# The attention output transposed by DMA instead of TensorE, and the output projection's half-depth products gathered four tiles at a time

## The chip, the core and the metric

The kernel runs on one core of a Trainium2 chip. The metric is the device time of one execution in microseconds (us). Three runs of the kernel before gave a median of 173.98 us (173.03 to 174.68).

## What is computed

One transformer block with two parallel branches on 2048 rows of width 448: linear attention with 16 heads of 28 channels and a softmax feature map, and a two-layer feed-forward net with the Mish activation. Both read the same normalized rows, and the block adds both to its input.

```
xn = layernorm(x)                                 # x: 2048 x 448
q, k, v = split(xn @ wqkv)                        # 16 heads x 28
pq, pk = q @ w_phi, k @ w_phi                     # per head 28 x 28
phi_q = [softmax(pq), softmax(-pq)]; phi_k likewise
kv = phi_k^T v;  z = sum(phi_k)
o = (phi_q @ kv) / (phi_q . z + 1e-6)
A = concat_heads(o) @ wo                          # 448 x 448
B = mish(xn @ w1 + b1) @ w2                       # 448 -> 1792 -> 448
out = x + A + B
```

## The kernel before, in words

The 2048 rows are 16 tiles of 128 rows. Names: TensorE is PE, VectorE is DVE, ScalarE is ACT, GpSimd is POOL; SP only issues DMAs. The program is written in one order, and a small planner (`Prog.add`) gives each engine its own in-order stream and puts a semaphore wait where an instruction needs what another engine or a DMA has produced, or a buffer or PSUM bank that another one still uses. Each DMA has a semaphore of its own. Nothing is reordered: an engine that waits holds up all that stands behind it.

The width 448 is three and a half times 128. A product over 448 channels is therefore cut into four chunks that start at channels 0, 128, 192 and 320 (`C0`), so that chunks 1 and 2 overlap in 64 channels. A tile uses three full chunks (`full`, L321) and 64 rows of the fourth (`rem`, L326). For two tiles of opposite parity the two half-depth products lie in different halves of the PE array, rows 0 to 63 and rows 64 to 127, and run side by side in a row-tiled pass. Where such a product stands between full products the array changes its tiling and back.

Three stages follow one another. In the first, layernorm, projections, exponentials and the sums over keys are computed; pairs of tiles are transposed on the way, the first two pairs on PE, the other six by DMA transposes from the SP queue (`xT`, L172). In the second, a loop over n = 0 to 27, PE computes the hidden layer: each n gives 128 hidden channels for 1024 rows (`ffn1_full` and, at every even n for two values of n, `ffn1_rem`), and ACT applies Mish (L491). Woven in, from n = 5 on, is the attention of tile m = n - 5: `nd_mm` (L438) multiplies exponentials of the queries with the key sums into two PSUM banks, one for each half of the feature map. The second half has a single bank, 7, for all tiles; the first half alternates between 5 and 6. `nd` then runs five DVE operations per tile: a reciprocal (L446), a product (L447), t2 (L449, the last to read bank 7), t1 (L452) and the reciprocal of the denominator (L454). POOL multiplies (L455) into one of four buffers `o_sb`. `t1` has two buffers.

`oTr(j)` takes a pair of tiles: eight PE transposes (L314) into PSUM bank 4, each of a 128 x 128 chunk, and one ACT copy (L463) into `oT`. `oT` is the memory of `EqT`'s first half, whose query exponentials have been read by then. The loop calls `oTr(0)` at m = 3, and so on every second step to m = 17 (n = 22).

In the third stage, `final(j)` for eight pairs of tiles, PE adds the second feed-forward layer (`f1`, L504: 14 products of 128 hidden channels each for a tile) and the output projection (three `full` products with `Wo` for each tile, and one side-by-side pass of the two `rem` products) in one PSUM bank per tile. DVE adds x (L515) into `out_sb`, and SP issues the store.

Of the kernel before, what the change touches and what calls it, by code (L numbers as in the profile page):

```python
# [5 lines left out]
ACT = mybir.ActivationFunctionType  # L6
ALU = mybir.AluOpType
# [5 lines left out]
D = 448  # L13
H = 16
DH = 28
F = 1792
P = 128
NT = S // P
FC = F // P
# [127 lines left out]
def ap_on(src, dims):  # L147
    return bass.AP(tensor=src.tensor, offset=src.offset, ap=[list(src.ap[0])] + [list(d) for d in dims])


def bass_parallel_sum__linear_kernel_hedgehog__dense_activation_mish__prompt_kernel(
    nc, A_x, A_wqkv, A_w_phi, A_wo, B_x, B_w1, B_b1, B_w2, out
):
    with ExitStack() as es:
        _kernel(es, nc, A_x[0], A_wqkv, A_w_phi, A_wo, B_w1, B_b1, B_w2, out[0])


def _kernel(es, nc, x2, A_wqkv, A_w_phi, A_wo, B_w1, B_b1, B_w2, out2):
    KC, KP, QG = 4, 112, 4
    E1 = DH + 1  # L160
    E2 = DH + 2
    pr = Prog(nc, es)
    pe = lambda fn, **k: pr.add("PE", fn, **k)
    act = lambda fn, **k: pr.add("ACT", fn, **k)
    dve = lambda fn, **k: pr.add("DVE", fn, **k)
    pool = lambda fn, **k: pr.add("POOL", fn, **k)

    def dma(eng, out, in_, r=(), w=()):
        return pr.add(eng, lambda e: e.dma_start(out, in_), r=r, w=w, dma=True)

    def dma_t(eng, out, in_, r=(), w=()):
        return pr.add(eng, lambda e: e.dma_start_transpose(out, in_), r=r, w=w, dma=True)  # L172

    def sb(name, shape, dtype=BF16):
        return es.enter_context(nc.sbuf_tensor(name, shape, dtype))

    ident = sb("ident", [P, P])
# [5 lines left out]
    x_all = sb("x_all", [P, NT, D])  # L183
# [5 lines left out]
    W2 = sb("W2", [P, FC, D])  # L189
    Wo = sb("Wo", [P, KC, D])  # L190
# [11 lines left out]
    hm = [sb(f"hm{i}", [P, FC, 1024]) for i in range(2)]  # L202
# [7 lines left out]
    t1 = [sb(f"t1_{i}", [P, H, E1], FP32) for i in range(2)]  # L210
    t2 = [sb(f"t2_{i}", [P, H, E1], FP32) for i in range(2)]
    rden = [sb(f"rden{i}", [P, H], FP32) for i in range(2)]
    NO = 4
    o_sb = [sb(f"o_sb{i}", [P, D]) for i in range(NO)]
    oT = EqT[:, 0, :, :]
    out_sb = [sb(f"out_sb{i}", [P, D]) for i in range(3)]
    PS = es.enter_context(nc.psum_tensor("PS", [P, 8, 512], FP32))
    PSb = PS.bitcast(BF16).rearrange("p (b n) -> p b n", b=8) if len(PS.bitcast(BF16).shape) == 2 else PS.bitcast(BF16)

# [11 lines left out]
    def wk(key):  # L231
        return [key + "0", key + "1"]
# [16 lines left out]
    for base, cm, st in ((0, 1, -DH), (DH - 1, -1, DH)):  # L249
# [7 lines left out]
         r=["wraw", "mask"], w=["Wbd"])  # L257
# [53 lines left out]
    def transp(e, bank, src, u):  # L311
        for c in range(KC):
            o = c * 256 + u * P
            i = e.transpose(PSb[:, bank, o:o + P], src[:, C0[c]:C0[c] + P], ident[:])  # L314
        return i
# [3 lines left out]
    def full(e, out, lhs, rhs, u, start=True, stop=False):  # L319
        for n, c in enumerate(FULL[u]):  # L320
            i = e.matmul(out, lhs(ALLP, c), rhs(ALLP, c), start=(start and n == 0), stop=(stop and n == 2))  # L321
        return i

    def rem(e, out, lhs, rhs, u, start=False, stop=True):
        h = slice(HP * u, HP * (u + 1))
        return e.matmul(out, lhs(h, 1 + u), rhs(h, 1 + u), start=start, stop=stop)  # L326
# [23 lines left out]
    def sl(w):  # L350
        return lambda h, c: w[h, c, :]
# [79 lines left out]
    def nd_bank(t, s):  # L431
        return 7 if s else 5 + t % 2

    def nd_mm(t, s):
        b = nd_bank(t, s)
        def f(e):
            for g in range(QG):
                i = e.matmul(PS[:, b, g * QG * E2:(g + 1) * QG * E2], EqT[0:KP, s, g, t * P:(t + 1) * P],  # L438
                             KVZ[:, s, g, :, :], start=True, stop=True)
            return i  # L440
        pe(f, r=[f"Eq{t // 4}{gp}{s}" for gp in range(2)] + [f"KVZa{s}", "KVZ1"], x=[b])

    def nd(t):
        i = t % 2
        nds = [PS[:, nd_bank(t, s), 0:H * E2].rearrange("p (h c) -> p h c", c=E2) for s in range(2)]
        dve(lambda v: v.reciprocal(rq[i][:, 1, :], nds[1][:, :, E1]), w=[f"rq{i}"], x=[7])  # L446
        dve(lambda v: v.tensor_tensor(rq[i][:, 0, :], nds[0][:, :, E1], rq[i][:, 1, :], ALU.mult),  # L447
            r=[f"rq{i}"], w=[f"rho{i}"], x=[nd_bank(t, 0)])
        dve(lambda v: v.tensor_tensor(t2[i][:, :, :], nds[1][:, :, 0:E1],  # L449
                                      ap_on(rq[i][:, 0, 0:1], [[1, H], [0, E1]]), ALU.mult),  # L450
            r=[f"rho{i}"], w=[f"t2{i}"], x=[7])
        dve(lambda v: v.tensor_tensor(t1[i][:, :, :], nds[0][:, :, 0:E1], t2[i][:, :, :], ALU.add),  # L452
            r=[f"t2{i}"], w=[f"t1{i}"], x=[nd_bank(t, 0)])
        dve(lambda v: v.reciprocal(rden[i][:, :], t1[i][:, :, DH]), r=[f"t1{i}"], w=[f"rd{i}"])  # L454
        pool(lambda g: g.tensor_tensor(o_sb[t % NO][:, :].rearrange("p (h d) -> p h d", d=DH), t1[i][:, :, 0:DH],  # L455
                                       ap_on(rden[i][:, 0:1], [[1, H], [0, DH]]), ALU.mult),
             r=[f"t1{i}", f"rd{i}"], w=[f"o{t % NO}"])

    def oTr(j):
        for u in range(2):  # L460
            t = 2 * j + u
            pe(lambda e, t=t, u=u: transp(e, 4, o_sb[t % NO], u), r=[f"o{t % NO}", "ident"], x=[4])
        act(lambda a: a.activation(oT[:, :, 256 * j:256 * j + 256],  # L463
                                   PSb[:, 4, :].rearrange("p (c n) -> p c n", c=KC), ACT.Copy),
            w=[f"oT{j}"], x=[4])

    def fargs(n, u):
        tcp, fc = n // FC, n % FC
# [2 lines left out]
    def ffn1_full(n, u):  # L471
        tcp = n // FC
        first = n % 2 == 0
        pe(lambda e: full(e, *fargs(n, u), u, first, not first),
           r=wk("W1") + [f"xT{4 * tcp + 2 * u}", f"xT{4 * tcp + 2 * u + 1}"], x=[2 * (n % 2) + u])

    def ffn1_rem(n):
        for i in (n, n + 1):
            pe(lambda e, i=i: (rem(e, *fargs(i, 0), 0, i > n, i == n), rem(e, *fargs(i, 1), 1, i > n, i == n))[1],
               r=wk("W1") + [f"xT{4 * (i // FC) + u}" for u in range(4)], x=[2 * (i % 2), 2 * (i % 2) + 1])  # L480
# [10 lines left out]
        act(lambda a: a.activation(hm[tcp][:, fc, :].rearrange("p (u n) -> p u n", u=2), PS[:, b:b + 2, :], ACT.Mish,  # L491
                                   bias=b1T[:, fc:fc + 1]), r=["b1T"], w=[f"hm{tcp}"] + rr, x=[b, b + 1])

    OB = [5, 0, 1, 2, 3, 6]
    def final(j):
        bs = [OB[(2 * j + u) % len(OB)] for u in range(2)]
        def wo(u):
            t = 2 * j + u
            return PS[:, bs[u], 0:D], sl(oT[:, :, t * P:(t + 1) * P]), sl(Wo)
        def f1(e, u):  # L500
            t = 2 * j + u
            for fc in range(FC):
                o = (t % 8) * P
                i = e.matmul(PS[:, bs[u], 0:D], hm[t // 8][:, fc, o:o + P], W2[:, fc, :],  # L504
                             start=(u == 0 and fc == 0), stop=(u == 1 and fc == FC - 1))
            return i
        pe(lambda e: f1(e, 0), r=[f"hm{j // 4}", "W2"], x=[bs[0]])
        pe(lambda e: full(e, *wo(0), 0, False, False), r=[f"oT{j}"] + wk("Wo"), x=[bs[0]])
        pe(lambda e: (rem(e, *wo(0), 0), rem(e, *wo(1), 1, True, False))[1], x=bs)
        pe(lambda e: full(e, *wo(1), 1, False, False), x=[bs[1]])  # L510
        pe(lambda e: f1(e, 1), x=[bs[1]])
        for u in range(2):
            t = 2 * j + u
            i = t % 3
            dve(lambda v, u=u, t=t, i=i: v.tensor_tensor(out_sb[i][:, :], PS[:, bs[u], 0:D], x_all[:, t, :], ALU.add),  # L515
                r=[f"x{t}"], w=[f"out{i}"], x=[bs[u]])
            dma("SP", ov[:, t, :], out_sb[i][:, :], r=[f"out{i}"])

    NP = NT // 2
    NWARM = 48  # L520
# [22 lines left out]
    def ln_b(j):  # L543
# [4 lines left out]
       r=["ident"], x=[7])  # L548
# [43 lines left out]
    for n in range(2 * FC):  # L592
        m = n - KV_END - 2
        if n:
            ffn1_full(n, 0)
        if 0 <= m < NT:
            nd_mm(m, 0)
        if n:
            ffn1_full(n, 1)
        if n % 2 == 0:  # L600
            ffn1_rem(n)
        mish(n)
        if 0 <= m < NT:
            nd_mm(m, 1)
            nd(m)
        if n == 0:
            for j in range(4):
                kv_mm(j)
        if 4 + n < NP:
            kv_mm(4 + n)  # L610
        if n == KV_END:
            kvz()
        if m >= 3 and m % 2 == 1 and (m - 3) // 2 < NP:
            oTr((m - 3) // 2)
    for j in range(NP):
        final(j)
    pr.finish()


# [26 lines left out]
```

## Time and profile before

| what | value |
|---|---|
| median of three runs | 173.98 us |
| the profiled execution: time, span | 174.11 us, 172.1 us |
| PE busy | 163.7 us, 95% of the span |
| DVE, ACT, POOL busy | 85.3, 81.7, 52.8 us |
| the attention steps in the loop, first to last `nd_mm` | 67.7 to 102.6 us |
| third stage | 114.5 us to the end |

The span is the part of the execution in which instructions run; 2.0 us lie outside it. Busy time says how long an engine had an instruction in work. For PE it is not the same as progress, since its products overlap one another and their ends are modelled; the chain of work that ended last gives each piece the time by which it moves the end. PSUM appears as PS. Because `oT` lies in `EqT`, the profile names it EqT; W in the third stage is W2, and in the second W1.

### The profile page before, as it was taken

The numbers are of one execution on the slowest core, as the hardware profiler recorded it, in microseconds if no ns is written. First come the engines' busy times: TensorE is split into PE (matmuls) and PEld (weight loads), VectorE is DVE, ScalarE is ACT, GpSimd is POOL, SyncE is SP. The second block draws the span as 40 slices with busy tenths as digits, with TensorE's granted clock in tenths as the row PEclk, the third lists the DMA queues.
The fourth block names the chain that finished last, engine by engine and source line by source line (L and its number), as shares of the span: only waits on it lengthen the run. The fifth ranks groups of instructions, "written<-read, shape, count | busy, mean of one in ns | idle before, by whom it ended". The sixth has DMA issues, their size and how long they took to land.

```text
span 172.1 us, 2723 instructions
## 1 busy us (share of the span) xinstructions
PE 163.7 (95%) x1137; PEld 85.0 (49%) x1137; DVE 85.3 (50%) x166; ACT 81.7 (47%) x84; POOL 52.8 (31%) x54
## 2 busy tenths in 40 slices
PE   6859899999999999999999999999999999999993
PEld 6734344444346855455555554344454544544541
DVE  1674966999996003898888883001121112111211
ACT  2374599999989535567766668760000000000000
POOL 5424259556699900244444442000000000000000
PEclk9987999999999999999999999999999999999999
DMA  5994693349900000000000000000000100110110
GB/s 159 360 234 73 213 228 98 61 35 314 258 0 4 0 2 4 0 0 4 0 0 0 4 0 0 0 4 27 27 27 31 51 28 27 50 32 27 30 52 28
DMA packets 15628, 10.72 MB, mean 62 GB/s; under 512 B 9216, under 2 KB 14848, under 8 KB 15616
## 3 DMA queue, kind: packets, MB, share of 16 engines
q1 hardware_dynamic: 14432, 9.15, 20.1%
q10 hardware_dynamic: 1152, 1.40, 2.4%
q8 instruction: 9, 0.15, 0.4%
q14 instruction: 3, 0.02, 0.1%
q0 software_dynamic: 32, 0.00, 0.0%
HBM read 6.68 MB, written 1.84 MB: 49 GB/s over the span
## 4 chain that ended last, share of the span: by engine, by line
PE 79%; DVE 9%; DMA 6%; ACT 4%; issue 1%; ACTq 1%; DVEq 0%
PE PS L321 35%; PE PS L504 25%; PE PS L326 7%; PE PS L438 4%; DVE xn L279 4%; PE PS L412 4%; DMA Wk<-in_A_wqkv_dram 3%; DMA xnT<-xn 2%; DVE Sk L392 2%; PE PS L314 2%; DVE stats L266 1%; ACT EqT L403 1%; ACT hm L386 1%; DVE Wp L309 1%; ACT hm L293 1%
## 5 line engine op out<-in xcount | busy, mean ns | idle before, releaser
L504 PE MATMUL PS<-W,hm 128*128 128x448 bf16 x224 | 43.8, 352 | 0.0
L321 PE MATMUL PS<-xnT,W 128*128 128x512 bf16 x168 | 43.0, 379 | 0.0
L491 ACT ACTIVATE hm<-PS,b1T 128x1024 bf16<-128x1024 f32 x28 | 31.2, 1113 | 20.5 <-PE PS L326 11.6
L515 DVE TENSOR_TENSOR out_sb<-PS,x_all 128x448 bf16<-128x448 f32 x16 | 10.0, 625 | 55.1 <-PE PS L326 33.5
L504 PEld LDWEIGHTS PS<-W,hm 128*128 128x128 bf16 x224 | 21.9, 98 | 20.5
L395 POOL TENSOR_TENSOR hm<-hm,rSk 128x1792 bf16<-128x1792 bf16 x8 | 25.5, 3211 | 8.8 <-DVE rSk L394 8.8
L321 PEld LDWEIGHTS PS<-xnT,W 128*128 128x128 bf16 x168 | 14.5, 97 | 11.6 <-issue 1.2
L392 DVE TENSOR_REDUCE Sk<-hm 128x64 f32<-128x1792 bf16 x8 | 15.9, 1992 | 1.5 <-ACT hm L386 1.5
L403 ACT ACTIVATE EqT<-PS 112x1024 bf16<-112x1024 f32 x16 | 15.4, 1022 | 0.3 <-PE PS L326 0.3
L386 ACT ACTIVATE hm<-PS 128x896 bf16<-128x896 f32 x16 | 13.9, 932 | 0.9 <-PE PS L321 0.9
L438 PEld LDWEIGHTS PS<-KVZ,EqT 112*128 112x128 bf16 x128 | 9.0, 97 | 9.1 <-DVE t_0 L452 3.0
L455 POOL TENSOR_TENSOR o_sb<-t_0,rden 128x448 bf16<-128x448 f32 x8 | 7.5, 940 | 19.3 <-DVE rden L454 19.3
L321 PE MATMUL PS<-xnT,Wp 128*112 128x512 bf16 x48 | 12.0, 385 | 0.9 <-ACT Wp L307 0.7
L438 PE MATMUL PS<-KVZ,EqT 112*128 112x120 bf16 x128 | 12.1, 216 | 0.0
L321 PE MATMUL PS<-Wv,xnT 128*128 128x448 bf16 x48 | 11.4, 378 | 0.4 <-DMA xnT<-xn 0.4
L321 PE MATMUL PS<-Wo,EqT 128*128 128x448 bf16 x48 | 11.8, 354 | 0.0
L279 DVE TENSOR_SCALAR xn<-x_all,mv,rstd 128x512 bf16<-128x512 bf16 x16 | 10.8, 718 | 1.2 <-POOL rstd L274 1.2
L455 POOL TENSOR_TENSOR o_sb<-t_1,rden 128x448 bf16<-128x448 f32 x8 | 7.5, 941 | 11.2 <-DVE rden L454 11.2
L266 DVE BATCH_NORM_STATS2 stats<-x_all 128x6 f32<-128x448 bf16 x16 | 9.1, 611 | 3.7 <-DMA x_all<-in_A_x_dram 3.7
L321 PE MATMUL PS<-Wp,xnT 128*128 128x448 bf16 x48 | 10.7, 359 | 0.0
L532 ACT ACTIVATE v_ext<-PS 128x896 bf16<-128x896 f32 x8 | 7.4, 919 | 5.5 <-PE PS L326 5.5
L321 PEld LDWEIGHTS PS<-xnT,Wp 128*112 128x112 bf16 x48 | 5.7, 129 | 6.7 <-ACT EqT L403 2.7
(62 smaller groups left out, 151.5 us busy)
## 6 DMA issues: line engine op xcount, KB each, us to landing
W<-in_B_w_dram SPq DMA_DIRECT2D x2, 896.0 KB, 5.3
out_dram<-out_sb SPq DMA_DIRECT2D x16, 112.0 KB, 1.7
W<-in_B_w_dram SPq DMA_DIRECT2D x1, 1568.0 KB, 7.7
x_all<-in_A_x_dram ACTq DMA_DIRECT2D x1, 896.0 KB, 7.9
x_all<-in_A_x_dram SPq DMA_DIRECT2D x2, 224.0 KB, 3.0
Wk<-in_A_wqkv_dram ACTq DMA_DIRECT2D x2, 224.0 KB, 4.6
Wv<-in_A_wqkv_dram SPq DMA_DIRECT2D x2, 224.0 KB, 5.9
x_all<-in_A_x_dram SPq DMA_DIRECT2D x1, 448.0 KB, 8.1
```

The lines of the kernel that those rows point to most:

```text
L266: dve(lambda v: v.bn_stats(stats[:, t, :], x_all[:, t, :]), r=[f"x{t}"], w=[f"st{t}"])
L279: eng(lambda v: v.tensor_scalar(xn[i][:, t % 2, :].rearrange("p (a b) -> p a b", a=2), ap_on(x_all[:, t, 0:1], [[192, 2], [1, 256]]), mv[: ...
L321: i = e.matmul(out, lhs(ALLP, c), rhs(ALLP, c), start=(start and n == 0), stop=(stop and n == 2))
L326: return e.matmul(out, lhs(h, 1 + u), rhs(h, 1 + u), start=start, stop=stop)
L386: act(lambda a, s=s: a.activation(Ek[j % 4][:, :, s, :], PS[:, 4:6, 0:D], ACT.Exp, scale=(1.0 if s == 0 else -1.0)), w=[f"Ek{j % 4}{s}"], ...
L392: dve(lambda v: v.tensor_reduce(Sk[b][:, :], Ek[q][:, :, :, :].rearrange("p t s (h f) -> p (t s h) f", f=DH), AX.X, ALU.add), r=[f"Ek{q}0" ...
L395: pool(lambda g: g.tensor_tensor(phik[:, 2 * j:2 * j + 2, :].rearrange("p t (k f) -> p (t k) f", f=DH), Ek[q][:, :, :, :].rearrange("p t s ...
L403: act(lambda a, s=s: a.activation(EqT[0:KP, s, 2 * gp:2 * gp + 2, tc * 512:(tc + 1) * 512], PS[0:KP, 6:8, :], ACT.Exp, scale=(1.0 if s == ...
L438: i = e.matmul(PS[:, b, g * QG * E2:(g + 1) * QG * E2], EqT[0:KP, s, g, t * P:(t + 1) * P], KVZ[:, s, g, :, :], start=True, stop=True)
L455: pool(lambda g: g.tensor_tensor(o_sb[t % NO][:, :].rearrange("p (h d) -> p h d", d=DH), t1[i][:, :, 0:DH], ap_on(rden[i][:, 0:1], [[1, H] ...
L491: act(lambda a: a.activation(hm[tcp][:, fc, :].rearrange("p (u n) -> p u n", u=2), PS[:, b:b + 2, :], ACT.Mish, bias=b1T[:, fc:fc + 1]), r ...
L504: i = e.matmul(PS[:, bs[u], 0:D], hm[t // 8][:, fc, o:o + P], W2[:, fc, :], start=(u == 0 and fc == 0), stop=(u == 1 and fc == FC - 1))
```

## The change

The transposes of `o` leave PE. POOL writes `o_sb` in the order of the overlapping chunks, 512 columns instead of 448: heads 0 to 8 (252 columns) from column 0 on, heads 7 to 15 from column 260 on, in one operation of 504 elements in place of 448 for each partition. The eight columns that are missing in between are copied from the same buffer by a second POOL operation. Then SP issues a DMA transpose of the whole tile (four blocks of 128 x 128) straight into `oT`, one for every tile, at the end of each step m = 0 to 15. The PE transposes and the ACT copies are gone. Since a DMA reads `o_sb` now, POOL's write of tile t waits until the transpose of tile t - 4 has landed.

`final` takes four tiles in place of two. The hidden products and full projection products of the first two tiles come first, then the half-depth products of all four tiles in one row-tiled pass (two side by side, and then two), then the rest of the last two tiles. It takes its PSUM banks from a ring of eight, and `out_sb` has four buffers.

```diff
-    o_sb = [sb(f"o_sb{i}", [P, D]) for i in range(NO)]
+    o_sb = [sb(f"o_sb{i}", [P, KC * P]) for i in range(NO)]
...
-        pool(lambda g: g.tensor_tensor(o_sb[t % NO][:, :].rearrange("p (h d) -> p h d", d=DH), t1[i][:, :, 0:DH],
-                                       ap_on(rden[i][:, 0:1], [[1, H], [0, DH]]), ALU.mult),
-             r=[f"t1{i}", f"rd{i}"], w=[f"o{t % NO}"])
+        ot = o_sb[t % NO]
+        hh = 9 * DH
+        pool(lambda g: g.tensor_tensor(ap_on(ot[:, 0:1], [[KC * P - hh, 2], [DH, 9], [1, DH]]),
+                                       ap_on(t1[i][:, 0, 0:1], [[7 * E1, 2], [E1, 9], [1, DH]]),
+                                       ap_on(rden[i][:, 0:1], [[7, 2], [1, 9], [0, DH]]), ALU.mult),
+             r=[f"t1{i}", f"rd{i}"], w=[f"oa{t % NO}"])
+        pool(lambda g: g.tensor_copy(ap_on(ot[:, hh:hh + 1], [[4, 2], [1, 4]]),
+                                     ap_on(ot[:, hh + 64:hh + 65], [[-124, 2], [1, 4]])),
+             r=[f"oa{t % NO}"], w=[f"o{t % NO}"])
...
-    def oTr(j):
-        for u in range(2):
-            t = 2 * j + u
-            pe(lambda e, t=t, u=u: transp(e, 4, o_sb[t % NO], u), r=[f"o{t % NO}", "ident"], x=[4])
-        act(lambda a: a.activation(oT[:, :, 256 * j:256 * j + 256], ...
+    def oTr(t):
+        dma_t("SP", oT[:, :, t * P:(t + 1) * P], o_sb[t % NO][:], r=[f"o{t % NO}", f"oa{t % NO}"], w=[f"oT{t}"])
...
-        pe(lambda e: f1(e, 0), r=[f"hm{j // 4}", "W2"], x=[bs[0]])
-        pe(lambda e: full(e, *wo(0), 0, False, False), r=[f"oT{j}"] + wk("Wo"), x=[bs[0]])
-        pe(lambda e: (rem(e, *wo(0), 0), rem(e, *wo(1), 1, True, False))[1], x=bs)
-        pe(lambda e: full(e, *wo(1), 1, False, False), x=[bs[1]])
-        pe(lambda e: f1(e, 1), x=[bs[1]])
+        for u in range(2):
+            pe(lambda e, u=u: f1(e, u), r=[f"hm{q // 2}", "W2"], x=[bs[u]])
+            pe(lambda e, u=u: full(e, *wo(u), u, False, False), r=[f"oT{ts[u]}"] + wk("Wo"), x=[bs[u]])
+        for v in range(2):
+            pe(lambda e, v=v: [rem(e, *wo(2 * v + u), u, v == 1, v == 0) for u in range(2)][1],
+               r=[f"oT{ts[2 * v + u]}" for u in range(2)], x=bs[2 * v:2 * v + 2])
+        evac(0)
+        evac(1)
+        for u in (2, 3):
+            pe(lambda e, u=u: full(e, *wo(u), u % 2, False, False), x=[bs[u]])
+            pe(lambda e, u=u: f1(e, u), x=[bs[u]])
+            evac(u)
...
-        if m >= 3 and m % 2 == 1 and (m - 3) // 2 < NP:
-            oTr((m - 3) // 2)
-    for j in range(NP):
-        final(j)
+        if 0 <= m < NT:
+            oTr(m)
+    for q in range(NT // 4):
+        final(q)
```

On PE, in the loop of the second stage at an even n from 8 to 22, the stream before and after (a minus marks what is gone; L326 are the half-depth products of the hidden layer):

```order
 L326 MATMUL PS<-xnT,W 128x512 x4
 L438 MATMUL PS<-KVZ,EqT 128x120 x4
-L314 MATMUL PS<-ident,o_sb 128x128 x8
 L321 MATMUL PS<-xnT,W 128x512 x3
 L438 MATMUL PS<-KVZ,EqT 128x120 x4
```

The eight transposes are taken out; at n = 20 and 22 they stand at the same place, with hidden-layer products behind them. Nothing else moves on PE in this loop.

On PE at the beginning of the third stage, before (L504 are the hidden products, L321 and L326 the full and half-depth products of the projection):

```order
L504 MATMUL PS<-W,hm 128x448 x14
L321 MATMUL PS<-Wo,EqT 128x448 x3
L326 MATMUL PS<-Wo,EqT 128x448 x2
L321 MATMUL PS<-Wo,EqT 128x448 x3
L504 MATMUL PS<-W,hm 128x448 x28
L321 MATMUL PS<-Wo,EqT 128x448 x3
L326 MATMUL PS<-Wo,EqT 128x448 x2
L321 MATMUL PS<-Wo,EqT 128x448 x3
```

and at the same place in the changed kernel, whose `f1` is on L508:

```order
L508 MATMUL PS<-W,hm 128x448 x14
L321 MATMUL PS<-Wo,EqT 128x448 x3
L508 MATMUL PS<-W,hm 128x448 x14
L321 MATMUL PS<-Wo,EqT 128x448 x3
L326 MATMUL PS<-Wo,EqT 128x448 x4
L321 MATMUL PS<-Wo,EqT 128x448 x3
L508 MATMUL PS<-W,hm 128x448 x14
L321 MATMUL PS<-Wo,EqT 128x448 x3
```

The number of products of each kind is unchanged. The half-depth ones stand in groups of four instead of two, and there are four such groups in place of eight.

On SP, from the last transpose of the first stage to the end of the program:

```order
 L172 DMA_TRANSPOSE xnT<-xn 128x8x128
 L169 DMA Wo<-in_A_wo_dram 128x2x448 x2
+L172 DMA_TRANSPOSE EqT<-o_sb 128x4x128 x16
 L169 DMA out_dram<-out_sb 128x448 x16
 L130 UNCONDITIONAL_BRANCH
```

The sixteen new transposes stand behind the load of `Wo` and ahead of all stores of the output.

More of the change, by code (lines that the diff above doesn't have):

```diff
@@ L213, in _kernel @@
     NO = 4
-    o_sb = [sb(f"o_sb{i}", [P, D]) for i in range(NO)]
+    o_sb = [sb(f"o_sb{i}", [P, KC * P]) for i in range(NO)]
     oT = EqT[:, 0, :, :]
-    out_sb = [sb(f"out_sb{i}", [P, D]) for i in range(3)]
+    out_sb = [sb(f"out_sb{i}", [P, D]) for i in range(4)]
     PS = es.enter_context(nc.psum_tensor("PS", [P, 8, 512], FP32))
@@ L454, in nd @@
         dve(lambda v: v.reciprocal(rden[i][:, :], t1[i][:, :, DH]), r=[f"t1{i}"], w=[f"rd{i}"])
-        pool(lambda g: g.tensor_tensor(o_sb[t % NO][:, :].rearrange("p (h d) -> p h d", d=DH), t1[i][:, :, 0:DH],
-                                       ap_on(rden[i][:, 0:1], [[1, H], [0, DH]]), ALU.mult),
-             r=[f"t1{i}", f"rd{i}"], w=[f"o{t % NO}"])
-    def oTr(j):
-        for u in range(2):
-            t = 2 * j + u
-            pe(lambda e, t=t, u=u: transp(e, 4, o_sb[t % NO], u), r=[f"o{t % NO}", "ident"], x=[4])
-        act(lambda a: a.activation(oT[:, :, 256 * j:256 * j + 256],
-                                   PSb[:, 4, :].rearrange("p (c n) -> p c n", c=KC), ACT.Copy),
-            w=[f"oT{j}"], x=[4])
+        ot = o_sb[t % NO]
[9 more added lines that the diff above has]
+        dma_t("SP", oT[:, :, t * P:(t + 1) * P], o_sb[t % NO][:], r=[f"o{t % NO}", f"oa{t % NO}"], w=[f"oT{t}"])
     def fargs(n, u):
@@ L492, in mish, with final @@
                                    bias=b1T[:, fc:fc + 1]), r=["b1T"], w=[f"hm{tcp}"] + rr, x=[b, b + 1])
-    OB = [5, 0, 1, 2, 3, 6]
-    def final(j):
-        bs = [OB[(2 * j + u) % len(OB)] for u in range(2)]
+    OB = [5, 6, 7, 4, 0, 1, 2, 3]
+    def final(q):
+        ts = [4 * q + u for u in range(4)]
+        bs = [OB[t % 8] for t in ts]
         def wo(u):
-            t = 2 * j + u
-            return PS[:, bs[u], 0:D], sl(oT[:, :, t * P:(t + 1) * P]), sl(Wo)
+            return PS[:, bs[u], 0:D], sl(oT[:, :, ts[u] * P:(ts[u] + 1) * P]), sl(Wo)
         def f1(e, u):
-            t = 2 * j + u
+            t = ts[u]
             for fc in range(FC):
@@ L504, in f1, with evac @@
                 i = e.matmul(PS[:, bs[u], 0:D], hm[t // 8][:, fc, o:o + P], W2[:, fc, :],
-                             start=(u == 0 and fc == 0), stop=(u == 1 and fc == FC - 1))
+                             start=(u < 2 and fc == 0), stop=(u >= 2 and fc == FC - 1))
             return i
-        pe(lambda e: f1(e, 0), r=[f"hm{j // 4}", "W2"], x=[bs[0]])
-        pe(lambda e: full(e, *wo(0), 0, False, False), r=[f"oT{j}"] + wk("Wo"), x=[bs[0]])
-        pe(lambda e: (rem(e, *wo(0), 0), rem(e, *wo(1), 1, True, False))[1], x=bs)
-        pe(lambda e: full(e, *wo(1), 1, False, False), x=[bs[1]])
-        pe(lambda e: f1(e, 1), x=[bs[1]])
[L512 to L515, printed above, removed]
+        def evac(u):
+            t = ts[u]
+            i = t % 4
+            dve(lambda v: v.tensor_tensor(out_sb[i][:, :], PS[:, bs[u], 0:D], x_all[:, t, :], ALU.add),
                 r=[f"x{t}"], w=[f"out{i}"], x=[bs[u]])
             dma("SP", ov[:, t, :], out_sb[i][:, :], r=[f"out{i}"])
+        for u in range(2):
[10 more added lines that the diff above has]
+            evac(u)
     NP = NT // 2
```

## The prediction

> **What bounds the kernel now.** I read the page's shares and slices first, then the chain of waits in order of time, then the timelines of the two places where the edits stand.
>
> ```profile
> PE 163.7 (95%) x1137; PEld 85.0 (49%) x1137; DVE 85.3 (50%) x166; ACT 81.7 (47%) x84; POOL 52.8 (31%) x54
> PE   6859899999999999999999999999999999999993
> DVE  1674966999996003898888883001121112111211
> PEclk9987999999999999999999999999999999999999
> PE 79%; DVE 9%; DMA 6%; ACT 4%; issue 1%; ACTq 1%; DVEq 0%
> ```
>
> PE is busy for nine tenths or more of every slice from the sixth (21.5 us on) until the last, at the full granted clock, and the chain that set the end is PE for 79%. But DVE is at 8 to 9 tenths in slices 16 to 23, where the attention of the sixteen tiles runs: a shorter PE there may meet DVE. So the chain has to be read stage by stage. Its columns are start, length and what ran:
>
> ```profile
> 70.48 0.54 PE PS L326 x4
> 71.02 0.32 PE PS L438 x4
> 71.98 0.21 PE PS L438 x4
> ...
> 74.57 0.54 PE PS L326 x4
> 75.42 0.45 PE PS L314 x8
> ...
> 79.10 0.54 PE PS L326 x4
> ...
> 106.20 0.55 PE PS L314 x8
> ```
>
> Two tiles make one round of this loop. The round from 70.48 to 74.57, in which no transposes stand yet, takes 4.09 us; the next, to 79.10, has eight and takes 4.53. The difference is 0.44 and the transposes' own piece is 0.45: they filled no wait, but pushed everything behind them. The last group shows 0.55 because it stands directly behind a row-tiled pass; the other 0.10 is the price of leaving that pass (0.32 against 0.21 in the two rows of L438), and the next product will pay it instead.
>
> The third stage, one pair of tiles, and the end:
>
> ```profile
> 118.70 5.30 PE PS L504 x28
> 124.00 0.57 PE PS L321 x3
> 124.57 0.30 PE PS L326 x2
> 124.86 0.67 PE PS L321 x3
> ...
> 169.20 0.03 issue
> ...
> 169.29 0.62 DVE out_sb L515
> ```
>
> It is PE alone, 6.84 us for a pair. A product of 448 columns takes 5.30/28 = 0.19. Two half-depth products side by side should take 0.19 as well but take 0.30, and the three full ones behind them 0.67 where those ahead take 0.57. So a change into the row-tiled form and back costs 0.11 + 0.10 = 0.21.
>
> **The change part by part.** *Transposes off PE.* Eight groups of 0.45 leave the chain: 8 x 0.45 = 3.6 us, if nothing else is late there. They cost 0.056 us each on the chain; this row gives the length of one:
>
> ```profile
> L314 PE MATMUL PS<-ident,o_sb 128*128 128x128 bf16 x64 | 4.9, 219 | 0.0
> ```
>
> The 219 ns is the latency of one, of which most overlaps its neighbours, so I take the chain's 0.45. The Trainium skill, "TensorE: Matmul & The Clock Gate", Part 4 (PE-mode transpose), gives about 275 ns for a 128 x 128 bf16 transpose inside a kernel; by that the sum would be an estimated 64 x 0.275 = 17.6 us, and the trace disagrees: back to back they advance the chain by 56 ns.
>
> *Is DVE late next?* Only six of the eight groups stand ahead of the last tile's `nd_mm`, so 2.7 of the 3.6 us has to be taken against DVE's five operations per tile. From the timeline of DVE and PE in the round without transposes:
>
> ```profile
> 71.37 0.26 DVE L446 RECIPROCAL rq<-PS 128x16 f32<-128x16 f32 x1 [0.26 <-PE PS L438]
> 71.87 0.64 DVE L449 TENSOR_TENSOR t_1<-PS,rq 128x464 f32<-128x464 f32 x1
> 72.57 0.32 PEld L438 LDWEIGHTS PS<-KVZ,EqT 112*128 112x128 bf16 x4 [0.22 <-DVE t_1 L449]
> 72.68 0.37 PE L438 MATMUL PS<-KVZ,EqT 112*128 112x120 bf16 x4
> 73.39 0.19 DVE L446 RECIPROCAL rq<-PS 128x16 f32<-128x16 f32 x1
> 75.46 0.26 DVE L446 RECIPROCAL rq<-PS 128x16 f32<-128x16 f32 x1
> 77.63 0.26 DVE L446 RECIPROCAL rq<-PS 128x16 f32<-128x16 f32 x1
> ```
>
> From 71.37 to 73.39 DVE had its input early (`nd_mm` ended at 72.68 + 0.37 = 73.05): saturated, a tile takes 2.02 us, so a round takes 4.04, just under PE's 4.09. The other hand-over is bank 7: `nd_mm` of a tile waits for the previous tile's t2, which ended at 72.51. The weight load began 0.06 later and the product 0.11 after that. That is the tightest spot, and PE's chain lost nothing there, for that round is the one of 4.09 us. In the following rounds the same offsets recur, as DVE starts an odd tile 0.04 behind PE each time. So I expect PE to stay the bound by a hair. The loss lies between 0 and 0.11 a round (the weight load no longer running ahead), for six rounds 0 to 0.7 us; I take 0, the value of the round seen.
>
> *ACT.* Eight copies go. What is left there, its Mish operations:
>
> ```profile
> L491 ACT ACTIVATE hm<-PS,b1T 128x1024 bf16<-128x1024 f32 x28 | 31.2, 1113 | 20.5 <-PE PS L326 11.6 <-PE PS L321 8.8
> ```
>
> ACT waits 20.5 us for PE ahead of its Mish operations, and one of 1.11 us falls into each 2.05 us, so this gains nothing and ACT does not become late.
>
> *POOL.* The product grows from 448 to 504 elements, and a small copy follows:
>
> ```profile
> L261 POOL CAST KVZ<-mask 112x32 bf16<-112x32 f32 x1 | 0.5, 540 | 0.0
> L245 POOL MEMSET mhalf<- 128x4 f32 x1 | 0.1, 101 | 0.0
> 71.19 0.94 POOL L455 TENSOR_TENSOR o_sb<-t_0,rden 128x448 bf16<-128x448 f32 x1 [10.93 <-DVE rden L454]
> ```
>
> By elements 0.94 x 504/448 = 1.06 us; the copy of eight elements lies between 0.10 and 0.54. Together 1.2 to 1.6 of the 2.05 us that a tile has. POOL only gives `t1` back, two tiles later, so this is hidden. Were the cover gone, the most it could add is 16 x 0.66 = 10.6 us, which needs POOL above 2.05 a tile.
>
> *The DMA transposes and their waits.* Behind SP's wait for POOL stand only later transposes and the stores:
>
> ```profile
> 43.09 1.13 SPq L169 DMA_DIRECT2D Wo<-in_A_wo_dram  x2
> 118.72 51.55 SPq L169 DMA_DIRECT2D out_dram<-out_sb  x16
> L172 SPq DMA_TRANSPOSE xnT<-xn x6: 1232/1242/1265, 14.5 to 41.8; - x6
> xnT<-xn SPq DMA_TRANSPOSE x1, 3.0
> xnT<-xn SPq DMA_TRANSPOSE x1, 5.8
> 28.00:30.00 2.00, 2.00 (x12) 0.94 (x12) 2.00 (x6) 1.72 (x4) 1.92 (x4) 1.00 0.00 0
> 30.00:32.00 2.00, 2.00 (x13) 0.90 (x10) 1.97 (x3) 2.00 (x3) 0.10 (x1) 1.00 0.65 127
> 32.00:34.00 2.00, 1.94 (x10) 0.89 (x8) 2.00 (x6) 2.00 (x3) 1.87 (x1) 1.00 0.02 4
> ```
>
> SP issues nothing from 44.2 to 118.7. A transpose of eight blocks costs its queue 1.24 us and lands 3.0 us after issue when alone, 5.8 beside a weight load (issues of two stretches). The stretches around 31 us (last columns: clock, DMA share, GB/s) show one alone: its traffic is all within 30 to 32 at a share of 0.65, 1.3 us of the DMA engines. The new ones have four blocks each, every 2.05 us, alone on the queues. POOL needs buffer t mod 4 again 4 x 2.05 = 8.2 us later; 1.6 + 3.0 = 4.6 (7.4 with the loaded landing) fits. The last lands at about 107 us (its tile's first reciprocal at 102.7 before, less 2.7, and 2 + 1.6 + 3.0 for the rest); the third stage, from 114.5 - 3.6 = 111 by the table of times, starts with the first. Their destination is strided, which the old ones' was not: no row prices that, and the rival below takes it up.
>
> PE now waits on sixteen DMA semaphores. A wait already met costs between 0 and the chain's "issue" piece of 0.03, 0 to 0.5 us; I take 0, as the first three projection products already had such a wait and take 0.57 = 3 x 0.19.
>
> *Third stage.* Eight changes of tiling become four: 4 x 0.21 = 0.84, say 0.8 us. The loop's groups of four suggest that a second pass adds only its own length: 0.54 for two passes of 512 columns against 0.30 here for one, 0.24 more, where a product of 512 columns by the 0.19 for 448 is 0.22. DVE's additions take 0.62 of 3.4 us a tile, and the end is unchanged: fourteen products, one addition, one store.
>
> Sum against the profiled execution: 174.11 - 3.6 - 0.8 = 169.7 us (span 172.1 to 167.7). It lay 0.13 above the median of 173.98, so 169.6.
>
> **The rivals.** *DVE becomes the bound.* If the spacing with a short wait, 77.63 - 75.46 = 2.17 us, is DVE's real pace, the last tile's reciprocal comes at best at 69.0 + 15 x 2.17 = 101.6, from this row and the first:
>
> ```profile
> 69.01 0.26 DVE L446 RECIPROCAL rq<-PS 128x16 f32<-128x16 f32 x1 [2.25 <-PE PS L438]
> 102.66 0.26 DVE L446 RECIPROCAL rq<-PS 128x16 f32<-128x16 f32 x1 [0.26 <-PE PS L438]
> ```
>
> against 102.7 before: 1.1 instead of 2.7 us, in all 1.1 + 0.9 + 0.8 = 2.8, so 171.2. Against it: the spacing of 2.02.
>
> *The tiling change is paid per pass.* Then a group of four saves nothing: 169.6 + 0.8 = 170.4. Against it is the loop's 0.54 for two passes.
>
> *The transposes only filled PE's waits*, so the edit does in the loop nothing for the time: 0.9 + 0.8 are left, 172.3. The 4.09 round speaks against it.
>
> *Slower: transposes are served one after another, each for its whole landing time P.* The tile 15 `nd_mm` needs t1 of tile 13, this POOL's tile 11, and that the transpose of tile 7. The first buffer is full at about 72.7, so this lands at 72.7 + 8P. After it come POOL's 1.06, DVE from the end of one t2 to the next tile's reciprocal (73.39 - 72.51 = 0.88) and from there to the end of that tile's t2 (72.51 - 71.37 = 1.14), and 0.17 for the weight load: 3.25 in all. The forecast has that `nd_mm` 0.4 ahead of its reciprocal, at 102.7 - 2.7 - 0.4 = 99.6. So nothing happens below P = 3.0 us; from 3.5 the gain of 4.4 is gone, from 3.7 it is over 1% slower. At 3.6 it gives 174.7, at 5.8 about 192. For it: the strided destination and the four blocks. Against it: 1.3 us of traffic for twice the blocks. The Trainium skill, "VectorE: DVE Perf Modes", The three transpose paths, gives 1309 ns for one 128 x 128 block by DMA, and its rules for kernel authors advise TensorE where PSUM is a possible destination; four blocks in a row would be an estimated 5.2 us, about 188 in all. The trace so far disagrees: eight blocks landed within 3.0 us.
>
> **How the numbers follow.** The forecast has 0.68; DVE 0.11, per-pass 0.09, filled waits 0.04, late transposes 0.08 (0.03 ending within 1%, 0.05 slower). A run within 1%, 1.74 us, can't be told from no change. Faster is 0.68 + 0.11 + 0.09 = 0.88, same 0.07, slower 0.05. The forecast's own range goes from 168.8 (the runs' spread below their median, 0.9) to 170.8 (0.7 + 0.5 of unknown costs); the first two rivals lift the upper end to 171.5.
>
> **What would show it.** Rounds of 4.09 us from 75 to 100; a tile's DVE spacing averaging 2.05; no idle PE ahead of L438; eight groups become four in the last stage, 13.5 us for four tiles; landings of 2 to 4 us; POOL at 1.2 to 1.6 a tile. It is wrong if rounds stay at 4.3 or more, if POOL waits for a DMA, or if the last stage still has 0.21 for each pair.

## The result and the profile after

The changed kernel takes 168.48 us (median of four, 168.11 to 168.63) against 173.55 us of the kernel before (median of four, 173.03 to 174.68): a ratio of 0.970, with a 95% interval from 0.964 to 0.975. Here and below a ratio leaves out runs that lie over 1.5% above the fastest of the same kernel. It is faster, as forecast, and by the forecast's mechanism. But the time lies 1.1 us below the forecast of 169.6 and 0.3 us below the range's lower end.

The page of the changed kernel, its shares, slices and chain:

```profile
PE 158.3 (95%) x1073; PEld 81.7 (49%) x1073; DVE 84.0 (50%) x166; ACT 74.5 (45%) x76; POOL 57.4 (34%) x70
DVE  1667958999995103599999992000410220211221
PEclk9999999999999999999999999999999999999999
PE 77%; DVE 10%; DMA 6%; ACT 4%; issue 1%; ACTq 1%; DVEq 0%
```

PE still carries the chain. DVE went from 8 or 9 tenths in the loop to 9 (90% or more). The clock row reads 9 in every slice; in the profile before, the second to fourth slices read 9, 8 and 7. The prediction shows that row, but reads it only from the sixth slice on.

The loop in the chain of waits:

```profile
69.39 0.54 PE PS L326 x4
...
73.48 0.54 PE PS L326 x4
...
77.56 0.54 PE PS L326 x4
...
98.00 0.54 PE PS L326 x4
```

Seven rounds lie between 69.39 and 98.00: 4.09, 4.08, and five more in 20.44, again 4.09 each. Every round now has the length of the one that had no transposes before. The chain holds no piece of DVE there. Four tiles of the last stage:

```profile
109.85 2.65 PE PS L508 x14
112.50 0.57 PE PS L321 x3
113.07 2.65 PE PS L508 x14
115.72 0.57 PE PS L321 x3
116.28 0.48 PE PS L326 x4
116.77 0.68 PE PS L321 x3
117.44 2.65 PE PS L508 x14
120.09 0.57 PE PS L321 x3
120.66 5.30 PE PS L508 x28
```

The pass of four half-depth products takes 0.48 where two passes of two took 0.60, and the dearer group behind a pass (0.68) comes once in four tiles. From 109.85 to 123.31 (halfway through the last row) that is 13.46 us for four tiles, against 2 x 6.84 = 13.68.

The new transposes and POOL's operations, by tile and by DMA issue:

```profile
L172 SPq DMA_TRANSPOSE EqT<-o_sb x16: 1188/1191/1494, 71.4 to 102.4; - x16
L457 POOL TENSOR_TENSOR o_sb<-t_0,rden x8: 1037/1039/1042, 70.1 to 98.9; 128x504 bf16<-128x504 f32 x8
L461 POOL COPY o_sb<-o_sb x16: 188/191/191, 71.2 to 102.2; 128x8 bf16<-128x8 bf16 x16
EqT<-o_sb SPq DMA_TRANSPOSE x16, 2.4
```

In the median they land 2.4 us after issue (the slowest 4.3), into a destination that is strided. POOL needs 1.04 + 0.19 = 1.23 us of a tile's 2.05. No engine waits for a transpose.

So where do the further 1.1 us come from? The first pieces of the chain that differ, before and after:

```profile
11.81 2.16 PE PS L321 x6
13.97 0.86 PE PS L326 x4
14.83 1.44 PE PS L321 x6
...
45.91 2.60 PE PS L321 x12
```

```profile
12.07 1.14 PE PS L321 x6
13.20 0.48 PE PS L326 x4
13.69 1.26 PE PS L321 x6
...
44.82 2.60 PE PS L321 x12
```

The same products take 4.46 us in the one and 2.88 in the other, and the common point at the end of the first stage comes 1.09 us earlier after the change, in a stage that the change doesn't touch. The stretch from 12 to 13 us shows what differs; its third column from the end is the granted clock of TensorE, first before, then after:

```profile
12.00:13.00 1.00, 1.00 (x4) 0.34 (x3) 1.00 (x4) 0.87 (x1) 0.22 (x1) 0.50 0.00 0
```

```profile
12.00:13.00 1.00, 1.00 (x8) 0.40 (x5) 1.00 (x5) 0.90 (x1) 0.02 (x1) 1.00 0.01 1
```

From that common point (the row of twelve products, L321) to the last addition the chain takes 169.29 - 45.91 = 123.38 us before and 163.78 - 44.82 = 118.96 after: 4.42 us less. The sum of the prediction was 3.6 + 0.84 = 4.44.

### The profile page after: what moved, and what is told of

The parts are those of the page before. It is cut to its first block, busy times and chain, and to the rows that moved or that the text cites. A ratio compares the mean times of both kernels' runs of the same rounds, so it can differ in the third digit from the quotient of the medians.

```text
span 166.6 us, 2631 instructions
## 1 busy us (share of the span) xinstructions
PE 158.3 (95%) x1073; PEld 81.7 (49%) x1073; DVE 84.0 (50%) x166; ACT 74.5 (45%) x76; POOL 57.4 (34%) x70
## 4 chain that ended last, share of the span: by engine, by line
PE 77%; DVE 10%; DMA 6%; ACT 4%; issue 1%; ACTq 1%; DVEq 0%
PE PS L321 35%; PE PS L508 25%; PE PS L326 7%; PE PS L438 5%; DVE xn L279 4%; PE PS L412 4%; DMA Wk<-in_A_wqkv_dram 3%; DMA xnT<-xn 3%; DVE Sk L392 2%; DVE stats L266 1%; ACT EqT L403 1%; ACT hm L386 1%; DVE Wp L309 1%; ACT hm L293 1%; ACTq L169 1%
## 5 line engine op out<-in xcount | busy, mean ns | idle before, releaser
L508 PE MATMUL PS<-W,hm 128*128 128x448 bf16 x224 | 44.5, 352 | 0.0
L321 PE MATMUL PS<-xnT,W 128*128 128x512 bf16 x168 | 43.0, 379 | 0.0
L492 ACT ACTIVATE hm<-PS,b1T 128x1024 bf16<-128x1024 f32 x28 | 31.2, 1115 | 24.2 <-PE PS L321 12.5
L508 PEld LDWEIGHTS PS<-W,hm 128*128 128x128 bf16 x224 | 21.9, 98 | 20.5
L321 PEld LDWEIGHTS PS<-xnT,W 128*128 128x128 bf16 x168 | 14.4, 97 | 12.1 <-issue 1.6
L457 POOL TENSOR_TENSOR o_sb<-t_0,rden 128x504 bf16<-128x504 f32 x8 | 8.3, 1039 | 15.8 <-DVE rden L454 15.8
L321 PE MATMUL PS<-xnT,Wp 128*112 128x512 bf16 x48 | 12.0, 385 | 0.9 <-ACT Wp L307 0.7
L321 PE MATMUL PS<-Wo,EqT 128*128 128x448 bf16 x48 | 11.7, 353 | 0.0
L321 PE MATMUL PS<-Wv,xnT 128*128 128x448 bf16 x48 | 10.4, 353 | 0.6 <-DMA xnT<-xn 0.6
L457 POOL TENSOR_TENSOR o_sb<-t_1,rden 128x504 bf16<-128x504 f32 x8 | 8.3, 1039 | 6.9 <-DVE rden L454 6.9
L321 PE MATMUL PS<-Wp,xnT 128*128 128x448 bf16 x48 | 10.5, 354 | 0.0
L321 PEld LDWEIGHTS PS<-xnT,Wp 128*112 128x112 bf16 x48 | 5.7, 129 | 6.7 <-ACT EqT L403 2.7
```

The costliest lines, as they stand in the source:

```text
L457: pool(lambda g: g.tensor_tensor(ap_on(ot[:, 0:1], [[KC * P - hh, 2], [DH, 9], [1, DH]]), ap_on(t1[i][:, 0, 0:1], [[7 * E1, 2], [E1, 9], [ ...
```

## The experiments

Two theories. A: the terms of the sum were right, and what lies beyond is the granted clock in the first stage, which differs by execution. B: the edits give more than was summed. The measure that tells them apart is the chain from the common point above to the last addition, since it leaves the first stage out; in the table it is called the rest.

| kernel | median us (runs) | mean clock 0.99 or less in | common point | rest |
|---|---|---|---|---|
| before | 173.42 (23) | 7 of 23 | 45.91 | 123.38 |
| before, again | 173.55 (12) | 3 of 12 | 45.08 | 123.39 |
| before, early idle time filled | 172.59 (12) | 0 of 12 | 44.72 | 123.38 |
| last stage in fours only | 172.98 (12) | 5 of 12 | 44.69 | 122.53 |
| DMA transposes only | 169.89 (6) | 2 of 6 | 46.63 | 119.81 |
| changed | 168.48 (4) | 0 of 4 | 44.82 | 118.96 |
| changed, again | 168.92 (6) | 2 of 6 | 45.53 | 118.96 |
| changed, early idle time filled | 167.94 (6) | 0 of 6 | 45.04 | 118.96 |
| changed, last stage in eights | 168.46 (6) | 3 of 6 | 45.69 | 118.53 |
| both of the two last | 167.67 (6) | 0 of 6 | 44.38 | 118.54 |

The medians and clocks are of all runs; common point and rest are of the one profiled execution. The rest repeats to 0.01 us, while the common point moves by 2.2 us. The clock is not all that moves it: unfilled kernels profiled at full clock have it between 44.69 and 45.98 (the last in an experiment further down), those with the dip between 45.69 and 46.63. A dip like the one in the profile of the kernel before, 1.7 of its 172.1 us lost, makes the mean clock 0.99.

**Each edit alone.** The DMA transposes with the last stage in pairs as before (the lines that differ from the changed kernel, in part):

```diff
-    for q in range(NT // 4):
-        final(q)
+    for j in range(NP):
+        final(j)
...
+        pe(lambda e: full(e, *wo(0), 0, False, False), r=[f"oT{2 * j}", f"oT{2 * j + 1}"] + wk("Wo"), x=[bs[0]])
...
```

> Only the transposes leave PE; the last stage works in pairs as before. Theory A (the terms of the prediction were right and the 0.7 us beyond them is the granted clock of the first stage, which is chance): 3.6 us off the kernel before at equal clock, a ratio of about 0.979, rounds of 4.09 us in the loop. Theory B (the edits themselves give more than was summed, and the surplus sits with the transposes): 4.3 us or more off, 0.975 or less, with the surplus visible between 45 us and the end.

The ratio is 0.979 (0.975 to 0.984). The rest is 3.57 us shorter, for 3.6 summed; there is no surplus in it.

The last stage in fours, with PE's transposes in pairs as before (against the kernel before, in part):

```diff
-    for j in range(NP):
-        final(j)
+    for q in range(NT // 4):
+        final(q)
...
+            pe(lambda e, u=u: full(e, *wo(u), u, False, False), r=[f"oT{ts[u] // 2}"] + wk("Wo"), x=[bs[u]])
...
```

> Only the last stage changes; the transposes stay on PE in pairs. Theory A: four changes of tiling saved, 0.8 us, ratio about 0.995; rounds of 4.53 us stay in the loop. Theory B with the surplus in the last stage: 1.5 us, ratio 0.991. If a change of tiling is paid per pass: no gain.

Its ratio, 0.998 (0.995 to 1.000), can't tell 0.8 us from nothing: five of its twelve runs had the lower clock. Its rest is 0.85 us shorter, for 0.84 summed. 3.57 + 0.85 = 4.42: the edits add without loss. The rival that a change of tiling is paid per pass is out.

**The clock.** Both kernels once more, unedited:

> The kernel before, unchanged. Theory A: its executions differ by about 1.4 us with the clock between 11 and 16 us: near 173.0 when it stays at full, near 174.3 when it falls to half there for 3 us; no part after 46 us differs. Theory B: all within 0.3 us of each other, and no such split.

> The changed kernel, unchanged. Theory A: 168.1 to 168.6 where the clock stays at full, and now and then 169.3 to 170 where it falls to half between 11 and 16 us. Theory B: always 168.1 to 168.6, the clock never falls.

Theory A holds for the span. In the 23 runs of the kernel before that all four experiments share, the sixteen with a mean clock of 0.998 or more have a median of 173.19 us, the seven at 0.99 one of 174.61: a low clock goes with 1.4 us more. In the other groups of runs of that kernel it is 1.7, 1.5 and 0.9 us, and two runs at full clock took 174.25 and 174.29 all the same, so a single time doesn't tell the clock. The profile of the kernel before, taken again, shows the clock at 1.00 from 12 to 13 us:

```profile
12.00:13.00 1.00, 1.00 (x6) 0.37 (x4) 1.00 (x5) 1.00 (x1) 0.14 (x1) 1.00 0.09 19
```

The changed kernel has the dip as well: two of the six new runs, at 169.44 and 169.65, against 168.41 to 169.07 of the other four. Its first four runs had none, by chance as far as ten runs can tell; the ten have a median of 168.62. With the dip they are where theory A had them (169.3 to 170); without it the spread is wider than expected, up to 169.07.

The dip follows a stretch in which PE waits for normalized rows. So 16 small products with an unread result were put there, in both kernels:

```diff
     ln_a(2)
+    pe(lambda e: [e.matmul(PS[:, 1, 0:P], ident[:], ident[:], start=True, stop=True) for _ in range(16)][-1],
+       r=["ident"], x=[1])
     xT(1)
```

> The kernel before with 16 small products whose result nobody reads put on PE where it waits for normalized rows (9.6 to 11.1 us). If the falling clock is PE's own idle time there: no run at a mean clock of 0.99, all between 172.5 and 173.7, median about 173.2. If the clock falls for a reason outside the program: one run in three still at 0.99 and above 174.

> The changed kernel with the same filling. Theory A: the median lies 4.4 to 4.7 us below the filled kernel before (4.4 in the span), the spread of both under 1 us, no clock of 0.99. Theory B: 5 us or more below it.

No run of the eighteen had the low clock, where before it was one in three or four. The PE timeline of the changed kernel, filled, shows the products in the gap:

```profile
9.70 0.57 PE L301 MATMUL PS<-Wbd,hm 112*128 112x112 bf16 x8 [0.35 <-ACT hm L293]
10.10 1.06 PE L572 MATMUL PS<-ident 128*128 128x128 bf16 x16
11.77 0.72 PE L339 MATMUL PS<-ident,xn 128*128 128x128 bf16 x8 [0.61 <-DVE xn L279]
```

The ranges are down to 172.06 to 173.06 and 167.60 to 168.57, with ratios to the kernel before of 0.995 (0.993 to 0.998) and 0.967 (0.963 to 0.971). Both medians lie 0.5 to 0.6 below those of the unfilled runs with a full clock; what besides the dip the filling saves was not looked into. Between the medians of the two filled kernels lie 4.65 us: 4.42 in the rest, and 0.25 that no span shows and theory A had not reckoned with. The time outside the span is 1.98 us on average in the filled kernel before and 1.73 in the filled changed one; it is 2.00 in the kernel before and 1.72 to 1.75 in the changed one, unfilled. What makes it shorter is not settled: in the experiments it went with the DMA transposes (1.74 with them alone, 1.98 with the fours alone), but a single run of the next kernel, which has them, shows 2.06.

**How late a transpose may be.** Two kernels test the dependence that priced the slow rival. In the first, each transpose waits until the one before has landed, since all of them write one name, "ch" (`oc` is an empty list):

```diff
-        dma_t("SP", oT[:, :, t * P:(t + 1) * P], o_sb[t % NO][:], r=[f"o{t % NO}", f"oa{t % NO}"], w=[f"oT{t}"])
+        dma_t("SP", oT[:, :, t * P:(t + 1) * P], o_sb[t % NO][:], r=[f"o{t % NO}", f"oa{t % NO}"] + oc, w=[f"oT{t}", "ch"])
```

> The changed kernel, each new transpose waiting until the one before has landed, so that they are served strictly in turn with P = 2.4 us and some tenths. The dependence that priced the slow rival (nothing happens below P = 3.0): rounds stay at 4.09 us, 121.8 us from the last transpose of the first stage to the end, although P is longer than the 2.05 us of a tile. If the buffers' ring followed at once: about 16 x 0.5 = 8 us more.

It takes 168.66 us (one run), with a rest of 118.95: nothing lost, although the transposes fall behind: the first is issued at 71.4 us and the last at 109.8 instead of 102.4, 38.4/15 = 2.56 us apart.

```profile
L172 SPq DMA_TRANSPOSE EqT<-o_sb x16: 1189/1190/1527, 71.4 to 109.8; - x16
  DMA EqT<-o_sb: 1.2, 1
```

The second row, from the same answer, is POOL's only wait for a landing. In the second kernel each transpose is done twice in that manner; this line is added behind the one above:

```diff
+        dma_t("SP", oT[:, :, t * P:(t + 1) * P], o_sb[t % NO][:], r=[f"o{t % NO}", f"oa{t % NO}"] + oc, w=[f"oT{t}", "ch"])
```

> The changed kernel, each transpose done twice in a row, each after the one before has landed: P of about 4.9 us for a tile. The price of the slow rival was 8 x (P - 3.0) = 15 us more, about 184; POOL would wait for the landing of the transpose four tiles back, and PE after DVE and POOL. If late transposes are hidden anyway: no change.

It takes 188.2 us (one run), with a rest of 138.74: 19.8 us more. The waits, and POOL's operations in the middle of the loop:

```profile
POOL o_sb L457 <- DMA EqT<-o_sb: 39.4, 11, 4.3
DVE t L452 <- POOL o_sb L457: 24.3, 8, 3.5
PE PS L438 <- DVE t L452: 10.4, 6, 2.6
87.05 1.04 POOL L457 TENSOR_TENSOR o_sb<-t,rden 128x504 bf16<-128x504 f32 x1 [4.27 <-DMA EqT<-o_sb]
...
117.47 1.04 POOL L457 TENSOR_TENSOR o_sb<-t,rden 128x504 bf16<-128x504 f32 x1 [4.11 <-DMA EqT<-o_sb]
```

That is the chain of the rival, transpose to POOL to DVE to PE. POOL's spacing from 87.05 to 117.47 is 30.42/6 = 5.07 us, by the formula 8 x (5.07 - 3.0) = 16.6. The other 3.2 are on PE behind the last of these waits, where the granted clock is 0.50:

```profile
110.00:120.00 10.00, 8.01 (x30) 2.93 (x30) 3.32 (x11) 2.31 (x3) 2.46 (x4) 0.50 0.27 54
```

The chain shows the last tile's `nd_mm` and the twelve products behind it, first in the changed kernel, then here:

```profile
97.14 0.21 PE PS L438 x4
...
98.85 2.59 PE PS L321 x12
```

```profile
113.92 0.58 PE PS L438 x4
...
117.26 4.05 PE PS L321 x12
```

From the common point (44.82 and 44.90) to this `nd_mm` it is 52.32 us in the one and 69.02 in the other: 16.70 more, the formula's wait. From there to the end of the twelve products it is 4.30 and 7.39: 3.09 more, which the formula left out.

**How near DVE is.** In one kernel PE gets less to do: the half-depth products of the hidden layer are left out from n = 6 to 21, so that part of that sum is missing.

```diff
-        first = n % 2 == 0
-        pe(lambda e: full(e, *fargs(n, u), u, first, not first),
+        first = n % 2 == 0 or 6 <= n <= 21
+        last = n % 2 == 1 or 6 <= n <= 21
+        pe(lambda e: full(e, *fargs(n, u), u, first, last),
...
-        if n % 2 == 0:
+        if n % 2 == 0 and not 6 <= n <= 20:
             ffn1_rem(n)
```

> The changed kernel without the half-depth products of the hidden layer from n = 6 to 21 (part of that sum is left out). PE then has about 3.45 us of work in a round, and what is left of the round is DVE's own pace. Forecast: 2.02 us a tile, rounds of 4.04. The rival in which DVE is the bound: 2.17 a tile, rounds of 4.34, which would be more than the 4.09 of the changed kernel.

It takes 167.58 us (one run). Now DVE is the chain in the loop, and these are its first operations of five tiles:

```profile
71.19 0.12 DVE rq L446
...
73.15 0.12 DVE rq L446
...
75.10 0.12 DVE rq L446
...
77.06 0.12 DVE rq L446
...
79.02 0.12 DVE rq L446
```

DVE's own pace is 7.83/4 = 1.96 us a tile, rounds of 3.92. The rival's 2.17 is out, and the forecast's 2.02 was a little high, so that the room below PE's 4.09 is 0.17 a round and not 0.05.

In the other kernel DVE gets more to do, the last reciprocal twice (`jk` is a buffer that nobody reads):

```diff
+        dve(lambda v: v.reciprocal(jk[:, :], t1[i][:, :, DH]), r=[f"t1{i}"])
         ot = o_sb[t % NO]
```

> The changed kernel with the reciprocal of the denominator done twice for each tile (0.25 us more on DVE). If DVE stands just behind PE (4.04 against 4.09 in a round): rounds of 4.04 + 0.5 = 4.5 us, 3 us more in all. If there is more room than that: less than 1 us.

It takes 168.41 us (one run). The rest is 119.15, only 0.19 longer; the 3 us were wrong. From the DVE timeline:

```profile
78.23 0.25 DVE L455 RECIPROCAL rden<-t 128x16 f32<-128x16 f32 x1
78.40 0.19 DVE L456 RECIPROCAL jk<-t 128x16 f32<-128x16 f32 x1
78.52 0.19 DVE L447 RECIPROCAL rq<-PS 128x16 f32<-128x16 f32 x1
80.58 0.19 DVE L447 RECIPROCAL rq<-PS 128x16 f32<-128x16 f32 x1
82.65 0.19 DVE L447 RECIPROCAL rq<-PS 128x16 f32<-128x16 f32 x1
```

The added reciprocal, whose input is ready, starts before the one ahead has ended, and the next one again before it has ended: it costs 78.52 - 78.40 = 0.12 us, not 0.25. A tile takes 2.07, a round 4.13 against PE's 4.09. The first three rounds of the chain still have 4.08 or 4.09; DVE falls behind from the fourth on, and four rounds of 4.13 to 4.15 make the 0.2 us. So the hand-over is tight after all: about 0.1 us of DVE a tile was the room.

**A step further.** The last stage in two groups of eight tiles:

```diff
-        ts = [4 * q + u for u in range(4)]
+        ts = [8 * q + u for u in range(8)]
...
-        for v in range(2):
+        for v in range(4):
...
```

> The changed kernel with the last stage in two groups of eight tiles, the half-depth products of all eight in one row-tiled pass. Two more changes of tiling gone: 2 x 0.21 = 0.4 us less than the changed kernel between 45 us and the end (121.4 instead of 121.8). If a long row-tiled pass loses something, or stores crowd at the end: no gain.

The rest is 118.53, 0.43 us less, for 0.42 expected. The pass of eight, in the chain:

```profile
123.59 0.86 PE PS L326 x8
124.45 0.67 PE PS L321 x3
```

Against one pass of two (0.30) each of the three further ones adds 0.19, its own length, and entering and leaving are paid once. With the filled idle time:

> The changed kernel with the last stage in two groups of eight and PE's early idle time filled with 16 small products. The two gains measured apart add: 167.94 of the filled changed kernel less 0.45 in the last stage, 167.5 us, no run at a mean clock of 0.99. If they overlap: 167.9.

167.67 us (167.08 to 168.12), a ratio of 0.965 (0.961 to 0.969) to the kernel before, no low clock, and the rest that eights alone have. The median is 0.27 below the filled changed kernel, where 0.45 was expected; their ranges overlap, so only the rest shows the gain of the eights here. It beats both kernels of this case.

## Why the prediction was right and where it was wrong

*Transposes off PE, 3.6 us.* Right: 3.57. The two neighbouring rounds of the chain, one with and one without transposes, were the right rows to take it from. The Trainium skill's 275 ns for a transpose ("TensorE: Matmul & The Clock Gate", Part 4) would have given 17.6; the 0.056 of the chain was right.

*DVE just not late.* Right, with more room than computed: in the changed kernel its tiles from 70.28 to 78.45 follow one another at 8.17/4 = 2.04 us, which is PE's pace, and its own is 1.96, not 2.02. The 2.02 came from a tile whose first reciprocal had waited for PE and then showed its whole length.

*Changes of tiling, 0.84 us.* Right: 0.85 alone, and 0.43 for two more.

*ACT, POOL and the transposes hidden.* Right. ACT now waits 24.2 us for PE ahead of its Mish operations (20.5 before), POOL needs 1.23 us a tile (1.2 to 1.6 forecast), the landing is 2.4 us (2 to 4 forecast). The slow rival's chain exists, but only where transposes are served in turn: 2.56 us apart nothing was lost, below its threshold of 3.0, and at 5.07 its wait came out as priced (16.7 us for 16.6), while the 3.1 us of PE at half clock were missing. Nothing was run between 2.56 and 5.07. The estimate of 5.2 us for four blocks from the Trainium skill's 1309 ns each ("VectorE: DVE Perf Modes", The three transpose paths) is too high here: they landed after 2.4. The advice of the same page (Rules for kernel authors) to transpose on TensorE where PSUM is a possible destination would have cost 3.57 us: TensorE was the engine that set the end.

*The step that failed* is the base of the sum, the 174.11 of "Sum against the profiled execution: 174.11 - 3.6 - 0.8 = 169.7 us" and the median of 173.98 behind it, taken as undisturbed. The prediction says of PE "at the full granted clock", but only from the sixth slice on, where that is so; it passed over the slices before, which read 9987. That execution had run at half clock from about 12 to 15 us. Of the three runs behind the median no clock is on record; the one of 174.68 lies above every run of this kernel with a full clock (at most 174.29), so it too very likely had the dip. By the 23 runs the base at full clock is 173.19, so the forecast should have been 173.19 - 4.42 = 168.8. The other term is the 0.25 us outside the span, which the prediction took as unchanged without naming it; its cause stays open. That makes 168.5, against 168.48 measured. How closely this agrees is luck: the four full-clock runs of the repeat have a median of 168.62, and with a dip or two among the first four of the changed kernel, too, the time would have come out higher.

The lower end of the range was the spread of the runs put below the forecast; it did not ask which of them was the undisturbed one. Nor does it come out as worked: the spread is 173.98 - 173.03 = 0.95, which gives 168.65 below 169.6, and not 168.8. The time lies below either.

The Trainium skill, "TensorE: Matmul & The Clock Gate", Part 1, says that the clock gate watches PE's activity in free-running windows of about 3.4 us which don't start with the kernel, so that the same kernel can meet them in another phase. That agrees with what the runs show, a stretch of about 3.4 us at half clock (0.12 + 3 x 0.50 + 0.09 us lost in the profile of before, by its stretches of 1 us from 11 to 16) in some of the executions and none in the others; no run here shows the window itself.

## What to carry to other kernels

A term that is read from two neighbouring rounds of the same chain, one with the work and one without, held here to a few hundredths; the base that it is taken from was 0.8 us off, so read the clock row of the profiled execution first and see from which of the runs the median comes. Compare kernels by a stretch between two common points when a stage ahead of it varies on its own. Here TensorE set the end and the DMA queues were idle, so the transposes were worth moving to DMAs as long as their buffers allowed the landing time, and the half-depth products were worth gathering, because a change of tiling was paid once per group.

## What the runs showed of the hardware that was not expected

- Issuing a transpose occupies SP's queue for 1.19 us with four blocks and 1.24 with eight: between these two it hardly depends on the size. The prediction read the 1.24 and had no row for four blocks; with sixteen transposes it is 19 us of SP's queue.
- A small DVE reciprocal that needs nothing of the one ahead began 0.12 to 0.17 us after it, where that one shows 0.19 to 0.25. The first reciprocal of a tile shows 0.26 us behind a wait for PE, and the product that reads it began 0.29 us after its start; without a wait it was 0.19 and 0.23.
- Gaps in PE's work of at most 1.5 us each, from 7 to 11 us, were enough for the clock to fall to half in some executions (1.4 us lost), and 16 small products in the last of them prevented that in all 24 runs of the three kernels that have them.
